# Dealing the kernel blocks of an S4D convolution anew between two feed-forward blocks, with a half's kernel products in single pieces

## The chip, the cores and the metric

The kernel runs on one core of a Trainium2 chip. The metric is the device time of one execution in microseconds; lower is better. A core has TensorE (PE, matmuls; PEld is its weight loads), VectorE (DVE), ScalarE (ACT), GpSimd (POOL) and SyncE (SP). All work at the same time, each through its own queue in order, and wait for each other by semaphores. SP and POOL also issue most of the transfers.

## The reference

One sequence of 2048 tokens with 576 channels goes through a convolution with a state-space kernel and then a feed-forward layer, each behind a layer norm with modulation. Cut to what matters:

```python
mod = (silu(c) @ w_mod).reshape(c.shape[0], 6, 1, -1)
sa, ca, ga, sb, cb, gb = (mod[:, i] for i in range(6))
h = layernorm(x) * (1 + ca) + sa
dt = exp(log_dt);  A = -exp(log_A_real) + 1j * A_imag
C  = (C_real + 1j * C_imag) * dt[:, None]
P  = exp((A * dt[:, None])[:, :, None] * arange(2048))
K  = 2 * einsum("dn,dnl->dl", C, P).real         # 576 kernels of 2048 taps
x  = x + ga * (causal_conv(h, K) + h * D_skip)
h  = layernorm(x) * (1 + cb) + sb
x  = x + gb * (relu(h @ w1) @ w2)                # w1 576 x 4608, w2 4608 x 576
```

All of it is float32. The kernel K needs, for each channel, a sum over 128 states for each of 2048 taps.

## The kernel before

**Blocks.** The tokens are four blocks of 512 (0 to 3). The convolution of block s needs the kernel's taps of blocks 0 to s. The feed-forward layer of a block is 36 steps, one for each 128 of the 4608 inner columns. A step is 14 matmuls into `hps` (L1326), a relu on ScalarE (`hh`, L1331) with its remainder on VectorE (`hl`, L1332), and 14 matmuls into `acc` (L1352) for the step before. Float32 matmuls are made of rounded high parts and low remainders, so each weight tile is split: in block 0 ScalarE copies the high part (`hi1` L1291, `hi2` L1301), VectorE subtracts for the low part (`lo1` L1296, `lo2` L1307 and L1308), and the low part is written out (L1408). Later blocks read the low parts back (L1280, L1311). The weights are read by SP (`load_r1` L1271 into two buffers, `load_r2` L1275 into three), and a buffer is free when its split is done.

**The kernel's taps.** The 576 channels are twelve halves of 48 channels (`NH = 12`; h = 0 to 5 make up the convolution's part 0, h = 6 to 11 part 1). For each half there is a table W2 (32 powers for each channel and state), a table W1 of 16 columns (coarser powers times C) and Z, the powers 512 and 1024. The taps of a half are products of W2 with W1, contracted over the 128 states. Block 0's taps come from W1 as it is (function `first`, ahead of the feed-forward layer). Those of blocks 1, 2 and 3 come from W1 rotated by 512, by 1024, and by both. `KGen.first` leaves W1, W2 and Z of all halves in DRAM, and `KGen.rest` takes them from there: `load0` (W0 and Z, three buffers) and `load2` (W2, two buffers) on POOL's queue, `rot` on VectorE (two products L481 and L483, two sums L485 and L487), `products` on TensorE (L515), an eviction on ScalarE (L525) into a tile `ker`, and after six halves `store` on SP's queue (L450). A rotation makes 16 columns, those of one block. The products of a half are 96 matmul calls, which the trace shows as 192 matmuls, in two halves of 6 q each with one PSUM buffer between them; a `yield None` after q = 2 cuts each half into two pieces of 48 matmuls.

**Who runs when.** While the feed-forward layer of block b runs, a generator makes what block b + 1 needs: block 0's makes kernel taps and then the convolution of block 1 (`conv(1)`), block 1's finishes block 0's output, makes kernel taps and then `conv(2)`, block 2's finishes and runs `conv(3)`. In `rest` the rotations of one half alternate with the products of the half before (`spread`). The generator is advanced four times a step, by `step(g)` at fixed places between the matmuls. Each `yield` gives a weight: the due time of VectorE work in us, None for a piece of TensorE work, -1 to end the call. A call goes on while the weights done so far are under a target (`rate(b)` times the calls made in the block), the VectorE weights of the last four calls are under `room`, and fewer than two pieces of TensorE were issued. A piece counts 0.35 in block 0 and 0.7 later. When a block's last step is issued, the rest of its generator is drained.

**Order.** `Kept` and `keep_in_program_order` fix an instruction's place in its engine's queue. The other instructions can be moved a little by the compiler's scheduler.

Before the change, block 0's generator takes the halves in the order 0, 6, 1, 7, ...; halves 0 to 5 get blocks 1, 2 and 3 (three rotations, 48 columns), halves 6 to 11 block 1 alone (one rotation, 16 columns). Block 1's generator takes halves 6 to 11 with blocks 2 and 3 (two rotations, 32 columns).

## Time and profile before

| | us |
|---|---|
| median of three runs | 1338.84 (1337.22 to 1343.99) |
| the profiled execution's own time | 1346.28 |
| its span, first to last instruction | 1344.5 |
| before the first relu of block 0 | 233.0 |
| block 0 of the feed-forward layer (from its first relu to block 1's) | 336.4 |
| block 1 | 277.0 |
| block 2 | 258.0 |
| block 3, up to 1333 us | 228.6 |

| engine | busy, us | share of the span |
|---|---|---|
| TensorE | 1218.3 | 91% |
| VectorE | 895.8 | 67% |
| ScalarE | 494.6 | 37% |
| GpSimd | 162.5 | 12% |

The mean granted clock of TensorE is 0.934. A row of the profile names line, engine, operation, what is written and read, shape and count; then busy time and mean duration; then the idle time of the engine just before and what ended it. A row of a table of stretches gives start and end, length, busy time of PE, PEld, DVE, ACT and POOL with the number of instructions, the granted TensorE clock, the share of the 16 transfer engines and their GB/s. A row of waits gives who waited for whom, the total in us, how often, and the longest. Matmuls overlap, so the time of one is read from start to start, not from its duration.

### The profile page before, as it was taken

How to read it: one execution, taken by the hardware profiler on the slowest of the kernel's cores; microseconds unless marked ns; L12 is line 12 of the kernel's file. 1: busy time of each engine (PE TensorE's matmuls, PEld its weight loads, DVE VectorE, ACT ScalarE, POOL GpSimd, SP SyncE). 2: the span in 40 equal slices, each digit the busy share in tenths (PEclk: the TensorE clock that was granted, in tenths of full speed). 3: DMA queues.
4: the chain of work that ended last, by engine and by line, in shares of the span. 5: the costliest groups of instructions: out<-in, count | busy, mean ns of one | idle time of the engine just before them, and what ended most of it. 6: DMA issues, size and time to landing. Idle time of an engine off the chain costs nothing.

```text
span 1344.5 us, 26011 instructions
## 1 busy us (share of the span) xinstructions
PE 1218.3 (91%) x10720; PEld 963.8 (72%) x10720; DVE 895.8 (67%) x1324; ACT 494.6 (37%) x863; POOL 162.5 (12%) x260
## 2 busy tenths in 40 slices
PE   4565686889989998999999999999999999999997
PEld 3344564667768676777777887887888888888885
DVE  5999978997995999768658995467996221111112
ACT  5688523222223422622234225433323352323331
POOL 0656501001100100011001000100000000000000
PEclk9556767999999998999999999999999999999998
DMA  8567972987878877698889995867996667666661
GB/s 269 218 231 291 307 272 80 346 298 273 320 279 288 297 247 290 206 400 322 281 276 339 346 357 160 275 219 271 349 392 189 176 178 230 193 197 199 199 177 53
DMA packets 122379, 345.85 MB, mean 257 GB/s; under 512 B 23916, under 2 KB 24212, under 8 KB 111508
## 3 DMA queue, kind: packets, MB, share of 16 engines
q1 hardware_dynamic: 105364, 226.96, 50.9%
q0 software_dynamic: 16384, 115.85, 23.0%
q8 instruction: 84, 1.38, 0.4%
q10 hardware_dynamic: 512, 1.38, 0.3%
q14 instruction: 35, 0.29, 0.1%
HBM read 262.73 MB, written 81.40 MB: 256 GB/s over the span
## 4 chain that ended last, share of the span: by engine, by line
PE 72%; DVE 14%; DMA 7%; issue 4%; ACT 2%; POOL 1%; ACTq 0%; POOLq 0%; DVEq 0%; SPq 0%
PE acc L1352 29%; PE hps L1326 28%; DMA r<-in_w_dram 4%; PE ps_f L846 4%; PE kps L71 2%; PE ph L71 2%; PE kps L515 2%; PE ps_i L1053 2%; DVE W1r L483 2%; DVE T L481 2%; DMA L2d<-w 1%; DVE W1r L487 1%; DVE W1r L485 1%; DVE T L62 1%; DVE w L1296 1%
## 5 line engine op out<-in xcount | busy, mean ns | idle before, releaser
L1326 PE MATMUL hps<-xh,w 128*128 128x512 f32 x1152 | 393.6, 402 | 1.9 <-issue 1.1
L1352 PE MATMUL acc<-w,hh 128*128 128x512 f32 x1152 | 370.6, 403 | 12.9 <-ACT hh L1331 12.9
L1332 DVE SCALAR_TENSOR_TENSOR hl<-hps,hh 128x512 fp32r<-128x512 f32 x144 | 99.1, 688 | 310.1 <-ACT hh L1331 309.3
L1352 PEld LDWEIGHTS acc<-w,hh 128*128 128x128 f32 x1152 | 216.3, 189 | 60.7 <-ACT hh L1331 14.5
L1326 PEld LDWEIGHTS hps<-xh,w 128*128 128x128 f32 x1152 | 218.5, 190 | 50.2 <-issue 1.6
L1326 PE MATMUL hps<-xl,w 128*128 128x512 f32 x576 | 229.7, 400 | 0.1
L1352 PE MATMUL acc<-w,hl 128*128 128x512 f32 x576 | 223.0, 399 | 0.9 <-DVE hl L1332 0.9
L1331 ACT ACTIVATE hh<-hps 128x512 fp32r<-128x512 f32 x144 | 85.8, 596 | 289.7 <-PE hps L1326 289.4
L1301 ACT ACTIVATE w<-r 128x576 fp32r<-128x576 f32 x141 | 96.7, 686 | 231.0 <-PE acc L1352 219.5
L1291 ACT ACTIVATE w<-r 128x640 fp32r<-128x640 f32 x140 | 102.7, 733 | 92.8 <-DMA r<-in_w_dram 92.8
L1326 PEld LDWEIGHTS hps<-xl,w 128*128 128x128 f32 x576 | 109.3, 190 | 23.9 <-DVE xl L47 0.6
L1352 PEld LDWEIGHTS acc<-w,hl 128*128 128x128 f32 x576 | 107.9, 189 | 24.7 <-DVE hl L1332 2.1
L1326 PE MATMUL hps<-xs,w 128*128 128x512 f32 x288 | 98.6, 413 | 0.0
L71 PE MATMUL kps<-W,W 128*32 128x16 f32 x2304 | 39.9, 211 | 45.3 <-POOL W L68 28.1
L1032 DVE TENSOR_TENSOR Y<-Y,T 128x1152 f32<-128x1152 f32 x60 | 79.4, 1351 | 0.0
L71 PEld LDWEIGHTS kps<-W,W 128*32 128x32 f32 x2304 | 35.1, 144 | 59.0 <-POOL W L68 30.8
L847 ACT ACTIVATE Z<-ps_f 128x288 f32<-128x288 f32 x120 | 48.8, 408 | 70.2 <-PE ps_f L846 68.8
L515 PEld LDWEIGHTS kps<-W1r,W2r 128*32 128x32 f32 x3456 | 44.7, 113 | 37.7 <-issue 19.0
L515 PE MATMUL kps<-W1r,W2r 128*32 128x48 f32 (+2 forms) x3456 | 52.1, 201 | 14.6 <-ACT ker L525 9.3
L1471 POOL DMA_DIRECT2D out_dram<-x x16 | 8.7, 544 | 468.6 <-DVE x L1463 466.3
L1326 PEld LDWEIGHTS hps<-xs,w 128*128 128x128 f32 x288 | 54.0, 191 | 11.3
L1352 PE MATMUL acc<-hl,w 128*128 128x512 f32 x144 | 56.7, 394 | 0.0
(235 smaller groups left out, 1586.6 us busy)
## 6 DMA issues: line engine op xcount, KB each, us to landing
r<-in_w_dram SPq DMA_DIRECT2D x144, 320.0 KB, 7.3
r<-in_w_dram SPq DMA_DIRECT2D x144, 288.0 KB, 5.1
w<-L1d SPq DMA_DIRECT2D x108, 320.0 KB, 3.2
w<-L2d SPq DMA_DIRECT2D x108, 288.0 KB, 2.8
W2r<-W2d POOLq DMA_DIRECT2D x18, 1536.0 KB, 9.2
W2d<-W SPq DMA_DIRECT2D x12, 1536.0 KB, 8.6
Ua<-Ud POOLq DMA_DIRECT2D x15, 1152.0 KB, 9.6
W<-W1d POOLq DMA_DIRECT2D x18, 768.0 KB, 10.6
```

Source lines behind the costliest of these rows:

```text
L71: self.tc.keep_in_program_order(self.nc.tensor.matmul(*args, **kw))
L481: v(T, X, zi, op=ALU.mult)
L515: nc.tensor.matmul(ps[32 * dd : 32 * dd + 32, q, :], W2[:, r, ch], W1[:, r, ch], start=(r == 0), stop=(r == 1),)
L846: nc.tensor.matmul(o, fc[:, n2, c, :], src(n2), start=True, stop=True)
L847: ev = nc.scalar.activation(Z[:, n2, c], ps[:, :PC], AF.Copy)
L1032: v(y, y, T, op=op or ALU.add)
L1291: copy(g - 1)(w1[g][:, 0], r1[g], AF.Copy)
L1301: copy(g)(w[:, 0:D], r2[g], AF.Copy)
L1326: nc.tensor.matmul(ps, a, x, start=(i == 0), stop=(i == 13))
L1331: nc.scalar.activation(hh, ps, AF.Relu)
L1332: nc.vector.scalar_tensor_tensor(hl, ps, 0.0, hh, op0=ALU.max, op1=ALU.subtract)
L1352: nc.tensor.matmul(acc[i], a, x, start=(f == 0 and seen[i] == 1), stop=(f == NF - 1 and seen[i] == (3 if i < 4 else 2)),)
```

## The change

Block 0's generator now makes blocks 1 and 3 for halves 0 to 5 and block 1 for halves 6 to 11; block 1's generator makes block 2 for halves 0 to 5 and blocks 2 and 3 for halves 6 to 11. Both take all twelve halves in sequence. There are 18 rotations in each block (before: 24 in block 0 and 12 in block 1), and block 3's columns come from block 1's rotated by 1024 in block 0, and from block 2's rotated by 512 in block 1. W1 always has 32 columns with two buffers, of which a half with one rotation uses 16. The tile `ker` has two buffers in block 0 and one in block 1. The `yield None` after q = 2 is gone, so a half's products are two pieces of 96 matmuls, and `spread` issues one after each 2n rotation operations, where n is the number of rotations. The target rates of blocks 0 and 1 are 1.74 and 2.1 instead of 2.15 and 1.8, the rooms 7.0 and 7.6 instead of 7.5 and 7.0.

```diff
-        hs = list(plan)
+        early = plan[0][0] == 1
...
-            def rots(h, W1, W0, Z):
-                blocks = plan[h]
-                a = [W1[:, :, :, 16 * i : 16 * i + 16] for i in range(len(blocks))]
-                if blocks[0] == 1:
-                    yield from rot(a[0], W0, Z, 0)
-                    if len(blocks) > 1:
-                        yield from rot(a[1], W0, Z, 1)
-                        yield from rot(a[2], a[0], Z, 1)
-                else:
-                    yield from rot(a[0], W0, Z, 1)
-                    yield from rot(a[1], a[0], Z, 0)
+            def rots(W1, W0, Z, n):
+                a = [W1[:, :, :, 16 * i : 16 * i + 16] for i in range(n)]
+                yield from rot(a[0], W0, Z, 0 if early else 1)
+                if n > 1:
+                    yield from rot(a[1], a[0], Z, 1 if early else 0)
...
-                blocks = plan[h]
+                blocks = plan[h // 6]
                 na = 16 * len(blocks)
                 if h % 6 == 0:
-                    ke[h // 6] = pt.tile([P, na, 72], F32, tag=f"ke{na}", bufs=1, name=f"ker_{h}")
+                    t = pt.tile([P, 32, 72], F32, tag="ke", bufs=1 + early, name=f"ker_{h}")
+                    ke[h // 6] = t[:, :na]
...
-                                    W1[:, r, ch],
+                                    W1[:, r, ch, :na],
...
-                        if q == 2:
-                            yield None
...
-                na = 16 * len(plan[h])
-                bufs = 1 if len(plan[h]) != len(plan[hs[i - 1]]) else 2
-                W1 = pt.tile([P, 2, H, na], F32, tag=f"W1{na}", bufs=bufs, name=f"W1r_{h}")
-                yield from spread(rots(h, W1, W0, Z), prev, len(plan[h]))
+                W1 = pt.tile([P, 2, H, 32], F32, tag="W1", bufs=2, name=f"W1r_{h}")
+                n = len(plan[h // 6])
+                yield from spread(rots(W1, W0, Z, n), prev, 2 * n)
...
-            yield from kg.rest(
-                self.cps, {h: (1, 2, 3) if h < 6 else (1,) for h in (0, 6, 1, 7, 2, 8, 3, 9, 4, 10, 5, 11)}
-            )
+            yield from kg.rest(self.cps, ((1, 3), (1,)))
...
-            yield from kg.rest(self.cps, {h: (2, 3) for h in range(6, NH)})
+            yield from kg.rest(self.cps, ((2,), (2, 3)))
...
-            room = (7.5, 7.0, 7.0, 7.0)[g // NF] - sum(recent[-3:])
+            room = (7.0, 7.6, 7.0, 7.0)[g // NF] - sum(recent[-3:])
...
-        return (2.15, 1.8, 1.4, 0.5)[b]
+        return (1.74, 2.1, 1.4, 0.5)[b]
```

More of the change, by code (lines that the diff above doesn't have):

```diff
@@ L457, in rest @@
         v = nc.vector.tensor_tensor
-        hs = list(plan)
+        early = plan[0][0] == 1
         with ExitStack() as ctx:
-            pt = k.pool(ctx, f"kr{len(hs)}", side="right")
+            pt = k.pool(ctx, f"kr{early}", side="right")
             d = Kept(k.tc, nc.gpsimd).dma_start
@@ L535, in products @@
                         )
-            nxt = [load0(hs[0])]
-            W2 = load2(hs[0])
-            nxt.append(load0(hs[1]))
-            for _ in range(1 if len(hs) == NH else 7):
+            nxt = [load0(0)]
+            W2 = load2(0)
+            nxt.append(load0(1))
+            for _ in range(1 if early else 7):
                 yield -1
             prev = iter(())
-            for i, h in enumerate(hs):
+            for h in range(NH):
                 W0, Z = nxt.pop(0)
-                if i + 2 < len(hs):
-                    nxt.append(load0(hs[i + 2]))
-                na = 16 * len(plan[h])
-                bufs = 1 if len(plan[h]) != len(plan[hs[i - 1]]) else 2
-                W1 = pt.tile([P, 2, H, na], F32, tag=f"W1{na}", bufs=bufs, name=f"W1r_{h}")
-                yield from spread(rots(h, W1, W0, Z), prev, len(plan[h]))
+                if h + 2 < NH:
+                    nxt.append(load0(h + 2))
+                W1 = pt.tile([P, 2, H, 32], F32, tag="W1", bufs=2, name=f"W1r_{h}")
+                n = len(plan[h // 6])
+                yield from spread(rots(W1, W0, Z, n), prev, 2 * n)
                 prev = products(h, W1, W2)
-                if i + 1 < len(hs):
-                    W2 = load2(hs[i + 1])
+                if h + 1 < NH:
+                    W2 = load2(h + 1)
             yield from prev
```

## The prediction

> **What bounds the kernel now.** I read the page first, then the busy time of each engine in the four feed-forward blocks (cut at the first relu of each block and at 1333 us), then the chain of waits, then who waited for whom, and last the rows of single instructions.

> ```profile
> span 1344.5 us, 26011 instructions
> PEclk9556767999999998999999999999999999999998
> ```

> ```profile
> core 0: us, PE busy (x) PEld busy (x) DVE busy (x) ACT busy (x) POOL busy (x), PEclk, DMA share, GB/s
> 233.00:569.40 336.40, 310.80 (x3441) 240.08 (x3440) 294.25 (x398) 105.07 (x199) 27.48 (x50) 0.96 0.79 284
> 569.40:846.40 277.00, 273.09 (x2259) 216.79 (x2258) 203.08 (x255) 95.92 (x177) 24.83 (x43) 1.00 0.86 307
> 846.40:1104.40 258.00, 258.00 (x1133) 209.29 (x1133) 165.26 (x231) 95.34 (x172) 12.35 (x22) 1.00 0.76 259
> 1104.40:1333.00 228.60, 228.60 (x1014) 189.43 (x1013) 31.73 (x48) 68.64 (x109) 2.17 (x4) 1.00 0.61 182
> ```

> Each block is 36 steps, and a step is 28 large matmuls. In block 3, where hardly anything else runs, the chain of waits is nothing but these:

> ```profile
> 1295.66 3.17 PE acc L1352 x14
> 1298.84 3.17 PE hps L1326 x14
> ```

> So a bare step takes 2 x 3.17 = 6.35 us, a matmul 0.227 us, and a bare block 36 x 6.35 = 228.6 us, which is block 3 to the last digit. Block 2 adds one convolution: 258.0 - 228.6 = 29.4 us of TensorE work (I take 28.5 for block 0, which has no output step). Blocks 0 and 1 also make kernel products (L515). The price of a piece is read where it cuts into the row of large matmuls: from the start of the matmul before it to the start of the one after it, less 0.227.

> ```profile
> 596.65 0.39 PE L1326 MATMUL hps<-xh,w 128*128 128x512 f32 x1
> 596.97 1.17 PE L515 MATMUL kps<-W1r,W2r 128*32 128x32 f32 x96
> 598.07 0.50 PE L1352 MATMUL acc<-w,hh 128*128 128x512 f32 x1
> ...
> 608.33 0.72 PE L515 MATMUL kps<-W1r,W2r 128*32 128x32 f32 x48
> ...
> 412.27 1.13 PE L515 MATMUL kps<-W1r,W2r 128*32 128x16 f32 x96
> ...
> 259.53 1.34 PE L515 MATMUL kps<-W1r,W2r 128*32 128x48 f32 x96
> ```

> 96 matmuls of 32 columns cost 598.07 - 596.65 - 0.23 = 1.19 us. By the differences of the durations, 48 of them cost 0.74 to 0.75, 96 of 16 columns 1.15, 96 of 48 columns 1.36 us. The set-up of a piece (about 0.3 us) weighs as much as a third of its matmuls, and the number of columns weighs little.

> Block 1 then adds up: 228.6 + 29.4 + 24 pieces x 0.75 = 276, against 277.0. TensorE is its bound. Block 0 does not: its twelve halves of three columns' worth (16.4 us) and twelve of one, in pieces of 48 (about 17.3 us), make 33.7, and 228.6 + 28.5 + 33.7 = 290.8 against 336.4. 45.6 us are missing there. Five stretches hold most of them:

> ```profile
> 245.00:252.00 7.00, 4.86 (x15) 3.54 (x14) 7.00 (x8) 2.48 (x4) 0.90 (x2) 0.76 1.00 409
> 292.00:303.00 11.00, 5.66 (x62) 4.31 (x61) 11.00 (x14) 1.36 (x3) 0.00 (x0) 0.69 0.93 346
> 319.00:327.00 8.00, 5.64 (x199) 4.00 (x198) 4.08 (x4) 1.74 (x3) 1.58 (x3) 0.79 0.41 137
> 394.00:406.00 12.00, 5.81 (x125) 3.93 (x128) 8.64 (x11) 2.83 (x5) 0.00 (x0) 0.72 0.60 223
> 521.00:532.00 11.00, 6.47 (x18) 4.81 (x18) 10.03 (x11) 2.67 (x5) 0.00 (x0) 0.69 0.57 223
> ```

> In each TensorE stands idle for 2 to 6 us (span less PE busy) and then runs some microseconds at half clock. At a granted 0.69 over 11 us, (1 - 0.69) x 11 = 3.4 us are lost to the clock alone. Idle plus clock is 3.8, 8.7, 4.1, 9.6 and 7.9 us, together 34.1. Why they happen:

> ```profile
> ACT w L1291 <- DMA r<-in_w_dram: 82.6, 19, 11.2
> PE acc L1352 <- ACT hh L1331: 12.9, 3, 6.2
> PE kps L515 <- ACT ker L525: 5.3, 1, 5.3
> SPq L1275 <- DVE w L1308: 191.2, 27, 14.0
> ```

> These rows are of block 0. ScalarE's queue is in order: the copy of a feed-forward weight (L1291) waits for its read, and the relu (L1331) or the eviction of kernel products (L525) that TensorE needs stands behind it. The read is late because the queue that issues it (SP) waited 191 us, in 27 waits, for VectorE's L1308, which frees the buffer. VectorE does that work behind the kernel's rotations. So in block 0 VectorE's backlog is what delays the reads. In block 1 no weight is split on VectorE any more, and its clock stands at 1.00.

> **The change, part by part.** *Six rotations move from block 0 to block 1* (block 2's kernel for the first six halves). A rotation is two products and two sums:

> ```profile
> L483 DVE TENSOR_TENSOR W1r<-W,Zr 128x1536 f32<-128x1536 f32 x18 | 31.3, 1750 | 9.6 <-PE kps L515 9.6
> L485 DVE TENSOR_TENSOR W1r<-W1r,T 128x768 f32<-128x768 f32 x24 | 22.7, 947 | 0.0
> ```

> 2 x 1.75 + 2 x 0.95 = 5.4 us, six are 32 us of VectorE. Block 0 falls from 294 to 262 us of it, block 1 rises from 203 to 235, still under TensorE's time there, so it is hidden. If that cover were gone, block 1 would pay the excess.

> *Pacing.* Four calls a step at 1.74 let 6.96 of the code's weights into a step of block 0; before, the room of 7.5 was the limit. Rotations and pieces weigh 18 x 5.4 + 24 x 0.35 = 105.6 and the convolution about 121, so the work ends after 227 / 6.96 = 33 of 36 steps, and nothing is drained at the block's end. In the first stage a step holds 6.4 us of rotations instead of about 7.6 (129.6 over some 17 steps). That is the relief of the backlog. In block 1, 280 of weights at 8.4 a step also end in step 33 to 34.

> *Products, block 0.* 12 pieces of 32 columns and 12 of 16: 12 x 1.19 + 12 x 1.15 = 28.1 instead of 33.7. TensorE's work becomes 228.6 + 28.5 + 28.1 = 285.2 us.

> *Products, block 1.* Twelve halves instead of six: 28.1 instead of 24 x 0.75 = 18, so +10.1. The 16-column price was read in block 0 at full clock; its bounds are 1.15 and, if one piece costs as much as two now, 1.5 (+14 instead of +10). Against this stands a wait that goes, since the two pieces of a half are now four or two VectorE operations apart and no longer share a step:

> ```profile
> PE kps L515 <- ACT ker L525: 3.9, 2, 2.7
> ```

> (block 1), so -3.9.

> [...]

> *Loads, block 1.* Six more halves bring six times three more issues on POOL's queue (W0, Z, W2), which is busy 25 of 277 us. What counts is their bytes:

> ```profile
> W2r<-W2d POOLq DMA_DIRECT2D x18, 1536.0 KB, 9.2
> W<-W1d POOLq DMA_DIRECT2D x18, 768.0 KB, 10.6
> Zr<-Zd POOLq DMA_DIRECT2D x18, 96.0 KB, 9.7
> ```

> ```profile
> 571.00:604.00 33.00, 30.56 (x225) 24.74 (x223) 22.75 (x21) 9.03 (x15) 6.00 (x12) 1.00 1.01 396
> ```

> 2.46 MB a half; the engines were full at 396 GB/s. A step's own weights are about 1.2 MB (block 3: 182 GB/s x 6.35 us). The first six halves of block 1 now have one rotation each: weight 5.4 + 2 x 0.7 = 6.8 of 8.4 a step, 0.81 steps a half. TensorE needs 0.81 x 6.35 + 2.3 = 7.5 us for that, the transfers (2.46 + 0.81 x 1.2) / 0.396 = 8.7 us. VectorE waits for a late load in order, and the relu's remainder (L1332) queues behind it, so the slower pace becomes the block's: 6 x 1.2 = 7 us. Bounds: 0 if the two halves loaded ahead cover it, 14 if each lack also costs half a clock window. [...] This trace shows 396 and even 409, so I stay with 7.

> *Loads, block 0.* The last six halves have one rotation too: 6.1 of 6.96, 0.88 steps, TensorE 7.9 us, transfers (2.46 + 1.06) / 0.396 = 8.9. The six lack 6 us; two are loaded ahead during the longer halves, so I take 4 (bounds 0 and 9).

> *The order of halves and the buffers.* Sequential halves with two W1 buffers take away VectorE's wait for products (9.6 us in the L483 row, on an engine that is full); that is within the relief above. In block 1 one ker buffer now serves both groups, so the seventh half's first eviction waits on ScalarE for the store of the sixth:

> ```profile
> kd<-ker SPq DMA_DIRECT2D x12, 288.0 KB, 5.9
> ```

> Four VectorE operations (5.4 us) lie between, so I take 0; at most 6 us once, with the relus behind it.

> *The stalls of block 0.* Those at 292 and 394 (18.3 us) fell in the stage whose VectorE load drops most; I take them as gone. The one at 245 (first loads of the block), at 319 (no wait shown) and at 521 (in the convolution) stay: 15.8. Of the unexplained 45.6 - 34.1 = 11.5 us I keep half, 6.

> **The sum.** Block 0: 285.2 + 15.8 + 6 + 4 = 311, which is 25.4 less than 336.4. Block 1: +10.1 - 3.9 + 7 = +13.2. Net -12. The profiled execution took 1346.3 us, 1.8 over its span, and lies 7.4 above the median of the runs, 1338.8; a difference carries over, so 1338.8 - 12 = 1327 us.

> **The rivals.** *Transfers, not VectorE, make the reads late (slower).* Place: the two stages of short halves, where demand passes 396 GB/s. For it: the stall at 245 came with the engines full (1.00, 409 GB/s). Against it: at 571 to 604 they were as full, and TensorE lost only 2.7 us. Then the five stalls stay: block 0 is 285.2 + 34.1 + 11.5 + 4 = 335, -1.6, block 1 still +13.2: 1350 us. It decides from the point where 12 of the 18.3 us stay.

> *The gain and the price cancel (no change).* The stalls stay because a weight read needs its 13 us whatever VectorE does, but the added loads are hidden: block 0 331 (-5.5), block 1 +6.2: 1340 us. For it: at 394 the stretch had only 0.60 of the transfers and still stalled.

> *All five stalls go (faster).* Block 0 285.2 + 11.5 = 297 (-39.7), loads hidden, block 1 +6.2: 1305 us. For it: VectorE has 32 us less in a stage where it was full. Against it: two of the five are not in that stage.

> *The single piece saves nothing,* since a piece of 96 costs what two of 48 do: 24 x 0.3 = 7 us more than the sum: 1334 us. Against it stands the row of 1.17 beside that of 0.72.

> **How the numbers follow.** The forecast has 0.42 and its own range is 1317 to 1337; slower 0.17; no change 0.22; all stalls gone 0.14; single piece 0.05. The range from 1306 to 1347 takes in all but the far ends of the first and third. About 0.5% (6.7 us) is what a measurement of this kernel can tell from no change. Faster than 1332: 0.32 of the forecast, 0.14, 0.05 of the cancelling case and 0.02, together 0.53. Within: 0.10 + 0.14 + 0.03 = 0.27. Slower than 1345.5: 0.17 + 0.03 = 0.20.

> **What would show it.** Right: block 0 near 311 us with two or three half-clock stretches, and SP's wait for L1308 well under 191 us; block 1 near 290 with the wait of kps on ker gone and its first kernel stage at 390 GB/s or more; pieces of 96 at 1.15 to 1.2 us throughout. Wrong: five stalls as before although VectorE has slack, which would mean that transfers set them; half-clock stretches in block 1; or a wait of ScalarE for the ker store.

## The result, and the profile after

The changed kernel is slower: a median of 1377.94 us (1373.33 to 1379.94, four runs) against 1338.18 (1337.22 to 1343.99, four runs). The ratio is 1.0283 with a 95% interval of 1.0244 to 1.0322. The forecast was 1327 us, with a range up to 1347. The profiled execution took 1379.94 us; it lies 33.7 us above the profiled one of before, 1346.28, and the medians lie 39.8 us apart.

From the page of the changed kernel, its span and its row of granted clock:

```profile
span 1378.1 us, 28385 instructions
PEclk9555788999999999989989999999999999999999
```

The busy times of the engines in the four blocks, cut as before (the last one at 1368 us):

```profile
core 0: us, PE busy (x) PEld busy (x) DVE busy (x) ACT busy (x) POOL busy (x), PEclk, DMA share, GB/s
232.60:558.20 325.60, 300.49 (x3416) 235.10 (x3415) 260.65 (x365) 101.42 (x193) 27.54 (x50) 0.96 0.81 291
558.20:881.50 323.30, 301.41 (x3437) 237.88 (x3436) 237.98 (x287) 102.68 (x195) 34.38 (x61) 0.96 0.86 312
881.50:1139.50 258.00, 258.00 (x1134) 209.27 (x1133) 165.24 (x231) 95.52 (x172) 12.37 (x22) 1.00 0.77 259
1139.50:1368.00 228.50, 228.50 (x1014) 189.34 (x1013) 31.63 (x48) 68.63 (x109) 2.19 (x4) 1.00 0.62 182
```

Blocks 2 and 3 are what they were. Block 0 fell by 10.8 us (forecast: 25.4) and block 1 rose by 46.3 (forecast: 13.2). Set beside the rows of before, TensorE alone tells most of it:

| | block 0 before | after | block 1 before | after |
|---|---|---|---|---|
| length, us | 336.4 | 325.6 | 277.0 | 323.3 |
| TensorE idle (length less busy), us | 25.6 | 25.1 | 3.9 | 21.9 |
| granted clock | 0.96 | 0.96 | 1.00 | 0.96 |

In block 0 TensorE idles as long as before, although VectorE has 34 us less to do. In block 1 it idles 18 us more, and 0.04 x 323.3 = 13 us more go to the clock. With the 10.1 us of added products that makes 41 of the 46.3. So the question is what TensorE waits for. The waits of block 0 in the changed kernel, with those of SP's queue last:

```profile
ACT w L1281 <- DMA r<-in_w_dram: 40.1, 9, 7.9
PE kps L510 <- issue: 16.8, 9, 4.5
PE kps L510 <- ACT ker L518: 5.3, 2, 5.0
...
SPq L1265 <- DVE w L1298: 166.7, 31, 11.6
```

and of block 1:

```profile
PE kps L510 <- issue: 16.8, 6, 3.8
ACT ker L518 <- DMA kd<-ker: 6.1, 1, 6.1
ACT w L1281 <- DMA r<-in_w_dram: 3.8, 3, 2.0
```

The waits of block 0 of which the forecast spoke did fall: ScalarE's wait for reads of weights from 82.6 to 40.1 us (on L1281, which was L1291), SP's wait for VectorE's split from 191.2 to 166.7. What took their place is "issue": 16.8 us in each block in which TensorE stood inside a piece of products and waited for nothing that the trace shows. Before, in block 0, the same row was:

```profile
PE kps L515 <- issue: 5.0, 4, 2.4
```

and block 1 had none. TensorE's instructions one by one, in the changed kernel's block 1 (start, length, line, count, and in brackets the idle time before):

```profile
593.47 1.13 PE L510 MATMUL kps<-W1r,W2r 128*32 128x16 f32 x96
594.53 0.74 PE L1316 MATMUL hps<-xs,w 128*128 128x512 f32 x2
595.20 0.43 PE L510 MATMUL kps<-W1r,W2r 128*32 128x16 f32 x20
598.65 1.29 PE L510 MATMUL kps<-W1r,W2r 128*32 128x16 f32 x76 [3.03 <-issue]
...
605.35 1.13 PE L510 MATMUL kps<-W1r,W2r 128*32 128x16 f32 x96
606.41 0.50 PE L1342 MATMUL acc<-w,hh 128*128 128x512 f32 x1
606.75 0.40 PE L1342 MATMUL acc<-w,hl 128*128 128x512 f32 x1
607.07 0.80 PE L510 MATMUL kps<-W1r,W2r 128*32 128x16 f32 x63
611.65 0.49 PE L510 MATMUL kps<-W1r,W2r 128*32 128x16 f32 x33 [3.78 <-issue]
```

An undisturbed piece of 96 takes 1.13 us, but two of these pieces stop in the middle, after 20 and after 63 matmuls, for 3.03 and 3.78 us. The places follow a count: from the first stop to the second there are 76 + 19 + 96 + 2 + 63 = 256 matmuls (19 large ones are in the lines left out), and 256 is 2 x 128. The page's row for the transfers of instructions (number of packets, MB, share), before the change and after it, shows the same unit:

```profile
q8 instruction: 84, 1.38, 0.4%
```

```profile
q8 instruction: 93, 1.52, 0.5%
```

These packets are 16 KB each (1.52 MB / 93). The change adds 1152 matmuls and nine packets: 128 matmuls with their weight loads, 256 instructions, to a packet. TensorE stops where a packet ends and the next one isn't there. If all the matmuls of the program are counted from its start, the stops inside products lie at nearly the same rest of a division by 128; the rest drifts slowly, presumably by other instructions and by records that are missing:

```
start us, length from start to start, matmul number, number mod 128
before  268.53  0.98   3278   78
before  319.71  2.57   4045   77
before  353.91  1.78   4683   75
after   312.46  1.68   4045   77
after   327.56  3.76   4300   76
after   348.91  4.71   4683   75
after   595.44  3.22   6724   68
after   607.69  3.96   6980   68
after   627.43  3.72   7363   67
after   706.43  3.87   8895   63
```

The stop at 319 in block 0 of before is one of them. The clock pays as well: in block 1 a stretch of 3.41 us or more at half clock begins in each of the stops of over 3 us or within a microsecond of its end, and the last of them falls into one that had already begun. (The first of the five half-clock stretches there, 588.27 to 591.68, follows another wait, of 1.85 us for an eviction.) The two stretches of block 1 that hold most products, in the changed kernel:

```profile
584.00:604.00 20.00, 15.11 (x416) 11.63 (x415) 16.36 (x13) 3.07 (x8) 3.17 (x6) 0.83 1.03 406
604.00:624.00 20.00, 15.79 (x425) 12.28 (x424) 11.44 (x10) 3.92 (x9) 2.74 (x6) 0.91 0.93 362
```

About 4.5 us of idle time in each 20, a granted clock of 0.83 and 0.91, and transfer engines that are full or nearly so: 1.03 of their time at 406 GB/s, then 0.93 at 362. Two reasons can stand behind the late packets, and the experiments separate them. *The packets' theory:* twice as many products in block 1, dealt out in bunches (up to 382 matmuls in one step), use a packet up in some 2 us, faster than the next can come. *The transfers' theory:* the added 14.8 MB of loads fill the transfer engines, and everything that is transferred comes late, the packets among it. The expectations call them Theory 1 and Theory 2. In both, "products" are the small matmuls of L510.

### The profile page after: what moved, and what is told of

Same layout as the page of the kernel before. It is cut to its first block, busy times and chain, and to the rows that moved or that the text cites. A ratio compares the mean times of both kernels' runs of the same rounds, so it can differ in the third digit from the quotient of the medians.

```text
span 1378.1 us, 28385 instructions
## 1 busy us (share of the span) xinstructions
PE 1232.5 (89%) x11872; PEld 976.6 (71%) x11872; DVE 897.3 (65%) x1324; ACT 498.2 (36%) x875; POOL 172.5 (13%) x278
## 3 DMA queue, kind: packets, MB, share of 16 engines
q0 software_dynamic: 18400, 130.60, 25.1%
q8 instruction: 93, 1.52, 0.5%
## 4 chain that ended last, share of the span: by engine, by line
PE 71%; DVE 11%; DMA 7%; issue 7%; ACT 2%; POOL 1%; SPq 0%; ACTq 0%; POOLq 0%; DVEq 0%
PE hps L1316 28%; PE acc L1342 27%; PE ps_f L836 4%; PE kps L510 4%; DMA r<-in_w_dram 4%; PE kps L71 3%; PE ph L71 3%; DMA Ua<-Ud 2%; DVE T L1020 1%; PE ps_i L1043 1%; DVE Y L1022 1%; POOL W L68 1%; DMA kd<-ker 1%; PE ps_t L1138 1%; DVE hl L1322 1%
## 5 line engine op out<-in xcount | busy, mean ns | idle before, releaser
L1342 PE MATMUL acc<-w,hl 128*128 128x512 f32 x576 | 231.9, 403 | 1.4 <-DVE hl L1322 1.0
L1291 ACT ACTIVATE w<-r 128x576 fp32r<-128x576 f32 x141 | 96.6, 685 | 237.5 <-PE acc L1342 233.6
L1316 PEld LDWEIGHTS hps<-xl,w 128*128 128x128 f32 x576 | 110.4, 192 | 25.1 <-DVE xl L47 1.7
L1281 ACT ACTIVATE w<-r 128x640 fp32r<-128x640 f32 x140 | 102.5, 732 | 44.1 <-DMA r<-in_w_dram 44.1
L510 PEld LDWEIGHTS kps<-W1r,W2r 128*32 128x32 f32 x4608 | 56.1, 116 | 65.8 <-issue 48.2
L510 PE MATMUL kps<-W1r,W2r 128*32 128x32 f32 (+1 forms) x4608 | 64.0, 197 | 41.9 <-issue 33.6
L71 PE MATMUL kps<-W,W 128*32 128x16 f32 x2304 | 40.8, 213 | 47.8 <-POOL W L68 28.1
L71 PEld LDWEIGHTS kps<-W,W 128*32 128x32 f32 x2304 | 35.9, 147 | 62.4 <-issue 31.6
L483 DVE TENSOR_TENSOR W1r<-W,Zr 128x1536 f32<-128x1536 f32 x24 | 42.1, 1752 | 31.6 <-PE kps L510 31.6
## 6 DMA issues: line engine op xcount, KB each, us to landing
r<-in_w_dram SPq DMA_DIRECT2D x144, 288.0 KB, 6.0
W2r<-W2d POOLq DMA_DIRECT2D x24, 1536.0 KB, 8.9
w<-L2d SPq DMA_DIRECT2D x108, 288.0 KB, 7.0
W2d<-W SPq DMA_DIRECT2D x12, 1536.0 KB, 8.8
W<-W1d POOLq DMA_DIRECT2D x24, 768.0 KB, 11.4
```

The lines of the kernel that those rows point to most:

```text
L71: self.tc.keep_in_program_order(self.nc.tensor.matmul(*args, **kw))
L483: v(out, X, zr, op=ALU.mult)
L510: nc.tensor.matmul(ps[32 * dd : 32 * dd + 32, q, :], W2[:, r, ch], W1[:, r, ch, :na], start=(r == 0), stop=(r == 1),)
L1281: copy(g - 1)(w1[g][:, 0], r1[g], AF.Copy)
L1291: copy(g)(w[:, 0:D], r2[g], AF.Copy)
L1316: nc.tensor.matmul(ps, a, x, start=(i == 0), stop=(i == 13))
```

## The experiments

For each run the time stands beside that of the kernel before on the same chip. For block 1 the table also gives the products' stage, from the block's first relu to the first one after its last product: its length over that of its bare steps (6.35 us each), and what is left of this when the pieces are taken off at their undisturbed price (1.19 us for 96 matmuls, 0.75 for 48). "Stops" are TensorE's waits for nothing shown in blocks 0 and 1, taken from start to start less 0.2 us and counted from half a microsecond on; the "issue" rows of the profile are taken otherwise, and give 16.8 us in each block of the changed kernel where the table has 16.2 and 17.9.

| run | us | before | block 0 | block 1 | stage over bare | less pieces | rest of block 1 over bare | stops |
|---|---|---|---|---|---|---|---|---|
| before (profiled) | 1346.28 | | 336.4 | 277.0 | 19.9 | 1.9 | 28.6 | 6.1 / 0 |
| after (profiled) | 1379.94 | | 325.6 | 323.3 | 62.9 | 34.3 | 31.8 | 16.2 / 17.9 |
| e1, change with pieces of 48 | 1377.76 | 1338.10 | 321.1 | 330.2 | 60.9 | 24.9 | 40.7 | 5.8 / 9.8 |
| e2, before with pieces of 96 | 1344.65 | 1338.10 | 334.1 | 279.5 | 21.4 | 7.1 | 29.4 | 6.3 / 2.4 |
| e3, change less 20 of 24 loads | 1342.94 | 1338.10 | 308.5 | 307.4 | 46.0 | 17.4 | 32.7 | 6.5 / 4.2 |
| e4, change with half the matmuls | 1343.05 | 1338.10 | 299.6 | 314.5 | 42.9 | 24.9 | 43.0 | 0 / 4.7 |
| e5, e1 with one piece to a call | 1376.20 | 1343.13 | 323.8 | 327.6 | 40.0 | 4.0 | 59.0 | 7.9 / 3.1 |
| e6, before with one piece to a call | 1357.54 | 1343.13 | 350.0 | 276.5 | 18.2 | 0.2 | 29.7 | 10.8 / 0 |
| e7, before, products of block 1 twice | 1384.12 | 1343.13 | 333.8 | 318.5 | 61.5 | | 28.4 | 6.5 / 7.9 |
| e8, before with more transfers | 1372.27 | 1343.13 | 337.2 | 299.4 | 42.2 | 24.2 | 28.6 | 6.6 / 0 |
| e9, e5 with higher rates | 1374.46 | 1341.72 | 324.3 | 327.6 | 48.9 | 12.9 | 50.1 | 12.5 / 3.2 |
| e10, e9 with pieces of 96 | 1376.08 | 1341.72 | 326.7 | 319.1 | 55.4 | 26.8 | 35.2 | 12.7 / 13.6 |
| e11, e5 with more room behind the products | 1367.23 | 1345.64 | 323.5 | 320.8 | 42.6 | 6.6 | 49.5 | 8.0 / 1.4 |
| e12, e11 less 20 of 24 loads | 1353.98 | 1345.64 | 310.3 | 318.0 | 40.0 | 4.0 | 49.4 | 2.1 / 0 |

The times of e1 to e12 are single executions, so a few us between two of them mean little. For e4, whose pieces have 48 matmuls, 0.75 us is taken off for each; for e7 nothing is, since its pieces have a price of their own (below).

### Is it the single piece? (e1, e2)

e1 puts the cut of the products back into the changed kernel, with one piece after each n rotation operations:

```diff
+                        if q == 2:
+                            yield None
...
-                yield from spread(rots(W1, W0, Z, n), prev, 2 * n)
+                yield from spread(rots(W1, W0, Z, n), prev, n)
```

> The changed kernel with the cut after q = 2 put back, and a piece taken after each n rotation operations instead of 2n, so that a half's products are again four pieces of 48. Theory 1 (TensorE runs out of its own instructions: they come in packets of 16 KB, 256 instructions, 128 matmuls with their weight loads, and the small matmuls use up a packet faster than the next one comes): the same number of instructions, but spread more evenly, so the idle time of L510 without a wait falls from 34 us to 10 to 20, with fewer half-clock stretches, against 24 x 0.3 = 7 us of TensorE work more; 1350 to 1365 us. Theory 2 (the added loads make data late): nothing changes in the loads, so the idle time stays and the 7 us are added: 1380 to 1388. If the cut itself was the protection of the kernel before, under 1345.

e2 does that part of the change alone, in the kernel before:

```diff
-                        if q == 2:
-                            yield None
...
-                yield from spread(rots(h, W1, W0, Z), prev, len(plan[h]))
+                yield from spread(rots(h, W1, W0, Z), prev, 2 * len(plan[h]))
```

> The kernel before with only the single piece: the cut after q = 2 is gone and a piece is taken after each 2n rotation operations. The plan, loads, rates and rooms are those of before. Theory 1: the total of instructions is that of before, block 1 has six halves of two rotations as before, so mild: the idle time without a wait of the products goes from 5 us to 5 to 15, and the pieces save up to 7 us: 1333 to 1348 us. Theory 2: the pieces save 5 to 7 us and nothing is lost: 1330 to 1334 us. If the single piece alone makes the change slow: over 1360.

The cut gives back nothing: 1377.76 us, in the range of neither theory. The stops fall as Theory 1 has it, from 34 to 15.6 us, but the pieces cost 7.4 us more in block 1, and the work left at its end is then drained with TensorE idle (the last step of the block takes 18.8 us against 7.5). Alone, the single piece costs before's kernel the 6.5 us by which this execution lies over its neighbour, or nothing against the profiled one (1346.28). The loss of 40 us comes from the rest of the change: the new dealing with its loads, buffers, rates and rooms, which were not tried one by one.

### Transfers or products? (e3, e4, e8, e7)

e3 leaves the loads of W0, Z and W2 out for ten of the twelve halves in both blocks; they work on the first two halves' data:

```diff
-                if h + 2 < NH:
-                    nxt.append(load0(h + 2))
+                nxt.append((W0, Z))
...
-                if h + 1 < NH:
-                    W2 = load2(h + 1)
+                if h == 0:
+                    W2s = [W2, load2(1)]
+                W2 = W2s[(h + 1) % 2]
```

> The changed kernel, in which only the first two halves of each of the two stages load W0, Z and W2, and the other ten use these again (the kernel taps of ten halves are therefore those of other channels; everything after them runs as before). 20 of 24 loads of 2.46 MB are gone, 49 MB. Theory 1 with a fetch whose time does not hang on the other transfers: the idle time without a wait stays near 34 us, 1360 to 1375. Theory 1 with a fetch that is slow because it queues behind the loads: it falls under half, 1335 to 1355. Theory 2: all goes, blocks 0 and 1 come near 300 and 290 us, 1320 to 1335; but then the gaps in the products would not fall on multiples of 128 matmuls.

e4 leaves out the second of the two products of each tap (r = 1), and so half of the products' matmuls:

```diff
-                            for r in range(2):
-                                nc.tensor.matmul(
-                                    ps[32 * dd : 32 * dd + 32, q, :],
-                                    W2[:, r, ch],
-                                    W1[:, r, ch, :na],
-                                    start=(r == 0),
-                                    stop=(r == 1),
-                                )
+                            nc.tensor.matmul(
+                                ps[32 * dd : 32 * dd + 32, q, :],
+                                W2[:, 0, ch],
+                                W1[:, 0, ch, :na],
+                                start=True,
+                                stop=True,
+                            )
```

> The changed kernel with only the r = 0 half of the kernel's products in blocks 0 and 1 (the real part of the sum; the imaginary part's matmuls are left out). Loads, rotations, evictions and pacing stay; a half has 96 matmuls in the trace instead of 192. TensorE's own work falls by 24 x 2 x 0.5 to 0.6, some 22 to 26 us in all. Theory 1: the packets are used up half as fast, the idle time without a wait falls from 34 to under 8 us and the half-clock stretches that follow it go (about 25 us of clock loss in blocks 0 and 1 falls to under 10): 1300 to 1320 us. Theory 2: only TensorE's work falls: 1350 to 1356 us.

Each brings the program back to 1343 us, and each takes most of the stops away: of 34.1 us 10.7 are left without the loads and 4.7 with half the matmuls. So as many stops need both. The time of e4 says little, though, and fell in the range of neither theory: TensorE is busy for 281.7 and 286.3 us in its two blocks, 33.9 us less than in the changed kernel, and that is nearly all of the 34.8 us by which the blocks got shorter. It idles as long as in the changed kernel (46 us in all against 47), since other waits took the place of the stops. Without the loads, the two blocks in e3:

```profile
227.30:535.80 308.50, 295.16 (x3415) 231.04 (x3414) 260.25 (x365) 101.30 (x193) 11.61 (x20) 0.99 0.66 227
535.80:843.16 307.36, 296.74 (x3437) 234.65 (x3436) 237.28 (x287) 102.81 (x196) 18.48 (x31) 0.98 0.72 248
```

TensorE's work is the same (3415 and 3437 matmuls), but it idles 13.3 and 10.6 us instead of 25.1 and 21.9, and block 0 is where the forecast had it (311). How long a packet takes to come tells more. I count from the first of the 128 matmuls that lead to a stop to the first one after it. In e3 all six stops follow 128 matmuls that took only 2.0 to 3.0 us, and TensorE goes on 2.8 to 5.3 us after their first. In the changed kernel seven of 15 stops are of this kind (3.1 to 6.8 us), and eight more come although the 128 matmuls took 3.7 to 8.2 us: there 5.9 to 9.5 us pass, five times of the eight with the transfer engines at 0.98 or more. The packet's own transfer takes 0.9 to 1.3 us in both, and each of these 21 stops ends 0.9 to 1.6 us after a packet has landed. What differs is when the transfer begins: 0.4 to 2.9 us after the first of the 128 in e3, 0.8 to 7.1 us in the changed kernel. So with the loads in place packets set out later, and with them gone delays of some 4 us are left, which only products in a row are fast enough to meet. Whether a packet stands behind other transfers or is asked for later isn't shown; how full the engines are in the single wait does not order the delays (3.1 us at a share of 1.01, 5.8 us at 0.70).

The page of e4 counts the packets once more:

```profile
q8 instruction: 75, 1.23, 0.4%
```

2304 matmuls fewer than after, 18 packets fewer: 128 each. Most of what was left in e4's block 1 was of another kind, the wait that the forecast had priced at nothing:

```profile
PE kps L509 <- ACT ker L517: 13.1, 3, 10.0
ACT ker L517 <- DMA kd<-ker: 5.8, 1, 5.8
```

One wait of 10 us, for an eviction that stood on ScalarE 5.8 us for the store of the first six halves out of the only `ker` buffer.

The other two runs add one cause each to the kernel before. e8 adds six times 2.3 MB of copies from DRAM to DRAM in block 1, one with each half:

```diff
+                if len(hs) < NH:
+                    d(out=k.Xd[h - 6][:, : 32 * H], in_=k.W1d[h - 6])
+                    d(out=k.Xd[h - 6][:, 32 * H :], in_=k.W2d[h - 6])
```

> The kernel before, in which block 1's generator moves 2.36 MB more for each of its six halves on the same queue (copies of W1 and W2 within DRAM that nothing reads), 14 MB in all as in the changed kernel. No instruction of TensorE is added. Theory 1: block 1 stays within 6 us of 277, no gaps without a wait, 1336 to 1345. Theory 2: block 1 is 13 to 40 us longer.

Block 1 takes 299.4 us, 22.4 more, as Theory 2 expected, and has no stop without a wait, as Theory 1 did. The price lies in late reads of weights. The block and its waits in e8:

```profile
574.72:874.10 299.38, 279.46 (x2259) 220.40 (x2258) 203.07 (x255) 96.00 (x177) 31.24 (x55) 0.97 0.89 331
...
ACT w L1295 <- DMA r<-in_w_dram: 39.7, 6, 15.2
PE kps L515 <- ACT ker L525: 15.1, 4, 8.0
```

So 14 MB of added transfers can cost 22 us in this block whatever the products do. They aren't quite the change's loads (these are spread over more halves, and read only), and in the changed kernel the wait for reads in block 1 is 3.8 us, not 39.7.

e7 issues each product of block 1 twice and adds no load:

```diff
-                            for r in range(2):
-                                nc.tensor.matmul(
...
+                            for again in range(2 if len(hs) < NH else 1):
+                                for r in range(2):
+                                    nc.tensor.matmul(
```

> The kernel before, in which block 1's products are each issued twice (the sums of block 1's generator come out doubled, which changes the kernel taps of blocks 2 and 3 for half of the channels; all later work runs the same). 1152 more matmuls, as in the changed kernel, with no more loads, rotations or evictions; a piece is 96 matmuls. Theory 1: besides 24 x 0.45 = 11 us of work, gaps without a wait appear in block 1, where there are none now, on multiples of 128 matmuls: 5 to 20 us, with half-clock stretches behind: block 1 295 to 315 us, the whole 1355 to 1375. Theory 2: only the 11 us: block 1 288, 1347 to 1351.

Three stops without a wait appear (7.9 us with half a microsecond's limit), at rests of 69, 68 and 67 by 128, where before had none: many products do this without any added load, though less than with it (17.9 us). As a measure of the change's price the run is spoilt: its products, with four calls in a row into the same 32 output partitions in place of two, cost more than was expected, and block 1 (318.5 us) and the program came out above Theory 1's ranges. TensorE in e7:

```profile
605.75 0.40 PE L1353 MATMUL acc<-hl,w 128*128 128x512 f32 x1
606.08 2.12 PE L516 MATMUL kps<-W1r,W2r 128*32 128x32 f32 x96
608.13 0.73 PE L1327 MATMUL hps<-xs,w 128*128 128x512 f32 x2
```

By the forecast's way of reading that is 608.13 - 605.75 - 0.23 = 2.15 us for 96 against 1.19. Most of the 41.5 us that e7's block 1 gained is this work: 24 pieces of 2.15 in place of 24 of 0.75 are 33.6 us.

### Spread out, does the loss go? (e5, e6, e9, e10, e11, e12)

If packets are late because products come in bunches, spreading should remove the stops with all the loads and all the products in place. e5 is e1 with the call ended after each piece, so that at most one piece of 48 is issued at each of the four places in a step:

```diff
             yield next(b, 0.0)
-    yield from b
+            yield -1
+    for w in b:
+        yield w
+        yield -1
```

> The changed kernel with pieces of 48 (the cut after q = 2, a piece after each n rotation operations) and at most one piece of products in a call of step: after each piece the call ends. So at most 4 x 48 matmuls of products come in a step of the feed-forward layer, where the changed kernel has up to 382. Plan, loads, rates and rooms stay. Theory 1 (TensorE's instructions come in packets of 128 matmuls, one after the other, each some 4 to 6 us after the one before was begun): the idle time without a wait falls from 34 us to under 8, 1335 to 1352 us. Theory 2 (the added loads): no change in their bytes or order, 1370 to 1385.

e6 has the same edit in the kernel before.

> The kernel before with the same limit of one piece of products in a call. Theory 1: its few gaps without a wait (6 us, with 10 us of half clock behind them) shrink, and the pieces that waited on the eviction of the piece just before them (kps on ker, 5.3 and 3.9 us) no longer do: 1322 to 1336 us. If the limit only delays work to the drained end of the block: 1340 to 1350.

e5's block 1 in three stretches, first the products, last the end of the block:

```profile
575.00:628.00 53.00, 50.26 (x1104) 37.52 (x1103) 33.38 (x28) 12.43 (x26) 7.93 (x15) 1.00 1.02 402
628.00:704.00 76.00, 76.00 (x1307) 58.52 (x1305) 65.03 (x55) 20.21 (x38) 7.49 (x13) 1.00 0.89 330
840.00:883.00 43.00, 28.15 (x93) 17.99 (x92) 31.49 (x58) 17.50 (x32) 0.00 (x0) 0.68 0.20 71
```

Where the products are, the loss is gone: the clock stands at 1.00 with the transfer engines as full as ever (1.02 at 402 GB/s), in the second stretch TensorE is busy for 76.00 of 76.00 us, and what is left above the pieces is 4.0 us instead of 34.3. But the program takes 1376.20 us, as the transfers' theory had it. Fewer pieces to a step put the convolution off, and at the end of the block its last part is drained in one step of 43.0 us, in which VectorE is busy for 31.5 us and TensorE for 28.2, partly in turn. e6 shows the same in block 0 of before: the last step takes 41.0 us (13.6 without the edit), and the program misses both ranges. It is this draining that the expectations of both runs left out or set too low. Pacing pays in one place and is paid for in another.

The next two runs raise the rates (to 1.9 and 2.6) and the rooms (7.6 and 9.0), with pieces of 48 in e9 and of 96 in e10. In both, and in e11 and e12, block 1's generator also begins its rotations three calls sooner (it ends four calls ahead of them, not seven):

```diff
-            for _ in range(1 if early else 7):
+            for _ in range(1 if early else 4):
...
-            room = (7.0, 7.6, 7.0, 7.0)[g // NF] - sum(recent[-3:])
+            room = (7.6, 9.0, 7.0, 7.0)[g // NF] - sum(recent[-3:])
...
-        return (1.74, 2.1, 1.4, 0.5)[b]
+        return (1.9, 2.6, 1.4, 0.5)[b]
```

> The changed kernel with pieces of 48, one piece to a call, as in the run before it of that kind, but with the two blocks' rates and rooms raised (1.9 and 2.6 a call, rooms of 7.6 and 9.0) so that the generators are done some two steps before the blocks end. If bunched products are what costs (they use up the packets of instructions faster than these arrive), the stretches of block 1 without a wait stay under 5 us, step 71 falls from 43.0 us to under 12, and block 1 ends near 228.6 + 29.4 + 24 x 0.75 x 2 = 294 plus 5 to 10 of waits, 299 to 304; the program near 1350. If the added transfers themselves set the pace, the higher rate only makes VectorE wait for late loads: block 1 stays above 315 and the program at 1365 or more, with no gain from the pacing.

> The same rates and rooms and one piece to a call, but pieces of 96 as in the change. Beside the run with pieces of 48 it tells what the single piece is worth once nothing is bunched. If bunching is the cause: 24 pieces in block 1 cost 24 x 1.19 = 28.6 in place of 36, so block 1 is some 7 us shorter than with pieces of 48 (292 to 297), and the program near 1342. If a piece of 96 is itself enough to run ahead of the packets, stretches without a wait come back in block 1 (10 us or more with half-clock windows) and it is as long as with pieces of 48 or longer. If transfers set the pace, both stay above 315.

Neither expectation held as a whole. Both blocks 1 stayed above 315, as the transfers' side had it, but not mainly for its reason (VectorE's waits for a late load come to 5.5 us in e9's products' stage). In e9 the stops stay away (3.2 us in block 1) and the drain shrinks only to 26.8 us: behind the products TensorE is busy for 127 us and VectorE for 110 of the 131 us up to the last step, and the convolution isn't done by then. In e10 nothing is drained (the last step takes 6.3 us), but the stops are back with 13.6 us, and 26.8 us lie above the pieces. A single piece of 96 is three quarters of a packet, and, as e10 shows, enough to run ahead of the packets even when paced. That answers e1 and e2: the length of the pieces matters, but what a shorter piece saves at the packets it gives back in set-up (7.4 us in e1's block 1) and at the block's end.

e11 is e5 with the earlier begin, a rate of 2.6 in block 1, and there a room of 7.6 for the first 18 steps and 8.6 after them:

```diff
-            room = (7.0, 7.6, 7.0, 7.0)[g // NF] - sum(recent[-3:])
+            room = (7.0, 7.6 if g < 54 else 8.6, 7.0, 7.0)[g // NF] - sum(recent[-3:])
...
-        return (1.74, 2.1, 1.4, 0.5)[b]
+        return (1.74, 2.6, 1.4, 0.5)[b]
```

> Pieces of 48, one to a call, with the changed kernel's own rate and room in block 0; in block 1 the room stays at 7.6 for the first 18 steps, where the products are, and is 8.6 after them, with a rate of 2.6 that no longer limits. Whether pacing repays the change: if the 43.0 us of step 71 were only work put off, the products' stage stays near 40 us over its bare steps, step 71 falls under 12, and block 1 ends near 300 (the program near 1350). If VectorE is full behind the products (its operations of the convolution took 6 to 9 us a step there), the put-off work can't be caught up: step 71 stays at 20 or more, block 1 at 312 to 322, the program at 1362 to 1372.

e12 is e11 with e3's edit: 20 of the 24 halves' loads left out.

> The same with 20 of the 24 halves' loads of W0, Z and W2 left out, so that the halves use the first two halves' data and the output is not the kernel's. Against the run before it only the transfers differ. If the packets of instructions, waiting behind transfers, and the weight reads make what is left of block 0's loss, block 0 falls by 12 to 18 us (to 306 to 312), as in the earlier run without these loads (325.6 to 308.5), and the stretches without a wait fall under 4 us in each block. If pacing alone had already removed what the transfers cost, both blocks stay within 4 us of the run with all loads. Block 1's products' stage, already near the sum of its work there, should fall by no more than 4 us in either case.

The two blocks of e11, and those of e12:

```profile
229.96:553.48 323.52, 305.55 (x3447) 237.66 (x3446) 266.03 (x375) 103.66 (x198) 27.47 (x50) 0.99 0.82 294
553.48:874.25 320.77, 307.54 (x3433) 236.03 (x3432) 239.77 (x287) 102.23 (x195) 34.29 (x61) 0.98 0.86 314
```

```profile
231.23:541.55 310.32, 303.17 (x3447) 235.82 (x3446) 265.94 (x375) 103.91 (x199) 11.62 (x20) 0.99 0.67 228
541.55:859.56 318.01, 306.68 (x3433) 235.66 (x3432) 239.23 (x287) 102.50 (x195) 18.45 (x31) 0.98 0.70 240
```

e11 is the fastest full version of the change, at 1367.23 us, and still 21.6 over its neighbour. The second expectation held: step 71 takes 26.4 us, block 1 320.8. Without the loads block 0 falls by 13.2 us, as expected. Block 1 falls by 2.8 only, because the paced products no longer wait for packets there (1.4 us of stops with the loads, none without). In the products' stage of block 1 spreading is thus worth more than taking the loads away (6.6 us left above the pieces against 17.4 in e3), but the end of the block takes most of that back. In block 0 spreading gains little: the loads cost 13 us there with paced products and 17 without.

## Why the prediction was wrong, point by point

**What bounds the kernel now.** The reading of block 0 was right as far as it went: reads were late behind VectorE's backlog, and with less of that backlog the waits fell. It went wrong at the stop of 319 ("no wait shown"), which was counted among the stalls that stay and not looked into. It was the only large sample, ahead of the change, of the wait that then decided. The group rows held more of it. After the change and before it:

```profile
L510 PE MATMUL kps<-W1r,W2r 128*32 128x32 f32 (+1 forms) x4608 | 64.0, 197 | 41.9 <-issue 33.6
```

```profile
L515 PE MATMUL kps<-W1r,W2r 128*32 128x48 f32 (+2 forms) x3456 | 52.1, 201 | 14.6 <-ACT ker L525 9.3
L71 PE MATMUL kps<-W,W 128*32 128x16 f32 x2304 | 39.9, 211 | 45.3 <-POOL W L68 28.1 <-issue 17.1
```

L71 makes products of the same kind ahead of block 0, 2304 of them, and there "issue" already took 17.1 us before the change.

**Products, block 1: +10.1.** This is the step that failed most: the sum has a price for a piece, and puts what TensorE waits for its own instructions at nothing. A piece of 96 costs what was forecast where nothing disturbs it (1.13 to 1.19 us), so the price was right and the bounds too. But it was read from single pieces with large matmuls on both sides, and it leaves out that 96 small matmuls are three quarters of a packet. Two pieces within a few microseconds use up one and a half packets, and the next one came 3 to 9.5 us after the one before it was begun where TensorE stood for it. Stops of 17.9 us and some 13 us lost to half clock came on top of the 10.1.

The large matmuls use the packets up slowly: 28 of them take 6.35 us, so 128 take some 29 us, and blocks 2 and 3, where TensorE is busy for 258.00 of 258.00 and 228.50 of 228.50 us, have no such stop. The small ones, at 11 to 12 ns each (96 in 1.06 us from start to start at 593.47), use a packet up in some 2 us.

**Loads, block 1: +7, bounds 0 and 14; block 0: +4, bounds 0 and 9.** Probably too small in block 1. Taking ten of twelve halves' loads away is worth 15.9 us there and 17.1 in block 0 (e3); but only six of block 1's twelve halves are new, and block 0 had all of its twelve before, so no run shows the price of the added loads alone. The working asked how long the loads take beside the steps' own weights, and not what else travels on the same engines. In block 1 most of the price went through the instruction packets (stops of 17.9 us with the loads, 4.2 without); with paced products it is 2.8 us. The half-clock stretches that the upper bound counts on last 3.41 or 6.83 us in block 0 of before (323.32 to 326.74, 296.02 to 302.84).

**The only `ker` buffer: 0, at most 6.** It cost ScalarE 6.1 us once, the upper bound.

**The wait of kps on ker: -3.9.** It stayed for the most part. The row in block 1 of the changed kernel:

```profile
PE kps L510 <- ACT ker L518: 3.0, 2, 1.9
```

The two pieces of a half lie further apart in the order, but the eviction between them can still be late: the longer of the two waits ends at 588.00, and there the eviction stood in ScalarE's queue behind a copy of a weight that had waited 2.01 us for its read. VectorE's wait for products, which was to go, grew:

```profile
L483 DVE TENSOR_TENSOR W1r<-W,Zr 128x1536 f32<-128x1536 f32 x24 | 42.1, 1752 | 31.6 <-PE kps L510 31.6
```

Over the whole trace it went from 10.4 to 31.6 us, and in block 0, of which the forecast spoke, from 9.6 to 17.5. While TensorE stands, the buffer that the next rotation writes isn't free, which is the forecast's chain turned round; how much of the rise comes from the stops was not measured.

**Products, block 0: -5.6.** Not settled: TensorE's whole busy time fell by 10.3 us with the same mean clock, that of the products by 2.5 (35.5 to 33.0).

**The stalls of block 0: those at 292 and 394 go, -18.3, and half of the unexplained 11.5.** The waits that made them went: TensorE's stops with a releaser fell from 19.8 to 8.4 us. The time did not, since stops without one rose from 6.1 to 16.2 in the same stage, where the same 2304 products now follow each other within 16 steps instead of 19.

**The rivals.** "Transfers make the reads late" (1350) was the nearest, with the right culprit and the wrong victim: the reads were less late than before, the instructions were later. It was also too cheap by 28 us. "The single piece saves nothing" (1334) was beside the point, since neither cutting the pieces in the change (e1) nor joining them in the kernel before (e2) moved the time by more than 7 us. The 13 us of a weight read in the second rival are one read on the chain of before (13.41 us from 511.69); at the stalls of 245 and 292 the read on the chain took 10.36 and 9.87, and the medians of the page are 7.3 and 5.1. In the first rival's argument, TensorE lost 2.4 us from 571 to 604 by the row shown (33.00 less 30.56), not 2.7; nothing hangs on it.

**What would show it.** Two of the signs named for "wrong" came: half-clock stretches in block 1 and ScalarE's wait for the `ker` store. The signs named for "right" that concern the mechanism came too (SP's wait fell, the pieces' price held), and show that a mechanism can be right and not decide.

**What stays open.** Why a packet that is transferred in about 1 us comes only after some 4 us even without the loads isn't settled: the runs show when it is transferred and when TensorE goes on (0.9 to 1.6 us after the transfer ended), not when it was asked for. The new rates and rooms were only raised further, never set back to those of before, so their share in the 40 us is open. And even with 20 of the 24 halves' loads left out and no stop in it (e12), block 1 takes 318.0 us, with 49.4 us over the bare steps behind the products, where before had 28.6: work put off to the block's end. Nor was it tried to give block 1 a second `ker` buffer beside pacing, or to move the convolution's start; most of the 26 us drained in e11 would have to go for the change to draw level.

## What to carry to other kernels

Small matmuls use up instructions as well as array time: here 128 of them with their weight loads were one packet of 16 KB, used up in some 2 us. Where about as many stand close together, compare their rate with the packets of instructions. The sign here was idle time that ends with "issue" inside a row of equal instructions, at a fixed distance in the count of all of the engine's matmuls (256 from the stop at 595.44 to that at 607.69), and more of it with the added loads in place (34.1 us of stops in blocks 0 and 1, 10.7 without most of them). Price a piece not only alone, but at the spacing that the new schedule gives it, and follow an unexplained stop in the trace of before until it has a cause. When work is spread to avoid such stops, look at what the spreading puts off, since here the end of the block paid it back.
